# Linear attention and a feed-forward layer on one core: weight halves moved to GpSimd, the values' loads joined, the first loads on two queues

## The chip, the core and the metric

The kernel runs on one core of one Trainium2 chip. The metric is the device time of one execution in microseconds (us), and lower is better. In the profile PE is TensorE, PEld its weight loads, DVE is VectorE, ACT is ScalarE, POOL is GpSimd and SP is SyncE.

## The reference

Two parts follow each other. A linear attention over 8 batches, 8 heads, 576 positions and 64 elements per head; its result, 4608 tokens of 512 elements, goes through a feed-forward layer of 512 to 2048 to 512.

```python
def phi(x):
    proj = np.einsum('bhsd,df->bhsf', x, w_phi)            # 128 features
    proj = proj - np.max(np.abs(proj), axis=-1, keepdims=True)
    return np.concatenate([np.exp(proj), np.exp(-proj)], axis=-1)
q_p, k_p = phi(q), phi(k)
kv = np.einsum('bhsf,bhsd->bhfd', k_p, v)
z = np.sum(k_p, axis=2)
num = np.einsum('bhsf,bhfd->bhsd', q_p, kv)
den = np.einsum('bhsf,bhf->bhs', q_p, z)[..., None] + 1e-06
x = (num / den)                                            # as (4608, 512)
h = x @ w_in
out = np.maximum(0.01 * h, h) @ w_out
```

All is in float32. The seeds' factors make q, k and w_phi larger than plain normal numbers would be, so the exponentials spread widely.

## The kernel before, in words

**Pairs.** Two heads are handled together as a pair: 8 batches of 4 pairs, 32 pairs in all. `k_phase(i)` turns the keys and values of pair i into the table `kv` (with z beside it: the values' tile has 66 columns per row, 64 of v and two of ones), and `q_phase(i)` uses that table for the queries and writes normalized tokens into `ring`, two batches of them. Pairs 0 to 3 have functions of their own (`first_k_phase`, `first_q_phase`), since all engines are still empty then. In pairs 4 to 7 ("nat" in the code) the products are plain float32; from pair 8 on each operand is split into a high and a low half in float32r, and three products replace one.

**The feed-forward layer.** Tokens are taken in 18 blocks of 256. `split` divides a block into halves xh and xl. `layer1(i, ft)` makes one of 16 slices of the hidden layer (128 of 2048) for one block: 12 matmuls of 256 columns, lines 595, 596 and 598. `layer2` multiplies the slice's halves gh and gl by the second weight: 3 matmuls of 512 columns for each half of the block, lines 615 to 617. The first two blocks run side by side, slice by slice, so that each weight is used twice as it comes.

**The weights' halves.** The weights arrive as 64-bit floats, two 32-bit words each, and float32 numbers are built from them on the chip. `load_weights` (line 164 on) has 32 steps of 128x512 numbers, w_in and w_out of 16 slices in turn, and each step does this: one DMA of 512 KB into a raw buffer, Abs on ACT (line 177), two TENSOR_SCALARs (lines 178 and 179) and one SCALAR_TENSOR_TENSOR (line 180) on DVE, one more activation on ACT (line 182), an add on DVE (line 183, printed as ISA or CUSTOM_DVE), then a copy that rounds to the high half h on ACT, and a subtraction that leaves the low half l on DVE. The last two go through helpers and are printed as lines 67 (CAST w0h, w1h) and 72 (w0l, w1l). The step's tile `ql` has two buffers and `kvl` one. The first ten steps take their raw weights into `ring`, two buffers in turn.

**What sets the order.** Nothing is ordered by hand. The program gives each part a priority (`PF` for pairs 0 to 3, then `PU`, `PA` for the attention stream, `PW` for the weights, 0 for the layers), and a scheduler that runs when the program is built lays down, engine by engine, a fixed order of instructions. Each engine then works its list from the top, and waits where an input isn't there. So any edit may move instructions anywhere.

**Loads.** SP issues all DMAs. At the start (lines 147 to 157) they are the keys of pairs 0 and 1, `bd` (w_phi twice, on the diagonal of a tile that GpSimd has zeroed, line 148), the values of pairs 0 and 1, then keys and values of pairs 2 and 3. The values of a pair take three DMAs (lines 142 to 144, later lines 195 to 197): eight blocks of 64 columns from `v`, and the last 64 positions twice from `vt`, for each half of the partitions. The tile `rv` has one buffer; each time it is taken anew, GpSimd writes its ones (line 198). `load_k(i + 1)`, which loads keys and values of the next pair, is called early in `k_phase(i)`, while the matmuls of pair i still have to read `rv` in pairs 4 to 7. In later pairs the values are split into `vhl` first, and `rv` is free from then on.

Of the kernel before, what the change touches and what calls it, by code (L numbers as in the profile page):

```python
# [9 lines left out]
F32 = mybir.dt.float32  # L10
# [4 lines left out]
ALU = mybir.AluOpType  # L15
AX = mybir.AxisListType

P = 128
# [12 lines left out]
NN = 8  # L31
NK = 8
BUFS = {"kk": 4, "pmk": 2, "eq": 2, "m4": 3, "m4n": 2, "g": 2, "gh": 2, "gl": 2, "qh": 2, "ql": 2, "dn": 2}
PBUFS = {"a": 3, "c": 1, "h": 2, "acc": 2}
# [9 lines left out]
@with_exitstack  # L44
def attention_moe_kernel(ctx: ExitStack, tc: tile.TileContext, q, k, v, vt, w_phi, w_in, w_out, out):
    nc = tc.nc
# [4 lines left out]
    def ct(shape, dt, name):  # L51
        return cp.tile(shape, dt, tag=name, name=name)

    def st(shape, dt, tag, name=None):
        return sp.tile(shape, dt, tag=tag, name=name or tag, bufs=BUFS.get(tag, 1))

# [7 lines left out]
    def copy_(key, o, i):  # L64
        e = pick(key) or "a"
        if e == "a":
            nc.scalar.copy(o, i)  # L67
        else:
            (nc.vector if e == "v" else nc.gpsimd).tensor_copy(o, i)  # L69

    def tt_(key, o, a, b, op):
        (nc.vector if pick(key) == "v" else nc.gpsimd).tensor_tensor(o, a, b, op=op)  # L72
# [50 lines left out]
    def part(x, i, shape):  # L123
        n = shape[0] * (shape[1] if len(shape) == 2 else 1)
        x = x[:, i : i + n]
        return x if len(shape) == 1 else x.rearrange("p (a b) -> p a b", b=shape[1])

    first_k, first_q = {}, {}

    def first_load_k(i):  # L130
        if i == 0:
            rk = st([P, S], F32, "rk")
            rv = st([P, 10, 66], F32, "rv")
        else:
            rk = part(fk[i], 0, [S])
            rv = part(fk[i], S, [10, 66])
        nc.sync.dma_start(rk, k[i])
        first_k[i] = rk, rv

    def first_load_v(i):  # L140
        rv = first_k[i][1]
        nc.sync.dma_start(rv[:, 0:8, 0:64], v[i])
        nc.sync.dma_start(rv[0:64, 8:10, 0:64], vt[i])
        nc.sync.dma_start(rv[64:128, 8:10, 0:64], vt[i])
        nc.gpsimd.memset(rv[:, :, 64:66], 1.0)

    tc.cur_priority = 2 * PF
    nc.gpsimd.memset(bd, 0.0)
    for j in range(2):
        nc.sync.dma_start(bd[64 * j : 64 * j + 64, F * j : F * j + F], w_phi)  # L150
    for i in range(2):
# [9 lines left out]
    def load_weights():  # L161
        n = 0
        for ft in range(NFT):
            for which, src in ((0, w_in), (1, w_out)):
# [19 lines left out]
                h, l = weight(which, "h", ft), weight(which, "l", ft)  # L184
                copy_("h", h, w)
                tt_("l", l, w, h.bitcast(F32), ALU.subtract)
                n += 1
# [3 lines left out]
    def load_k(i):  # L191
        rk = st([P, S], F32, "ks" if i < NK and i % 2 else "rk")
        rv = st([P, 10, 66], F32, "rv")
        nc.sync.dma_start(rk, k[i])
        nc.sync.dma_start(rv[:, 0:8, 0:64], v[i])
        nc.sync.dma_start(rv[0:64, 8:10, 0:64], vt[i])
        nc.sync.dma_start(rv[64:128, 8:10, 0:64], vt[i])
        nc.gpsimd.memset(rv[:, :, 64:66], 1.0)  # L198
        kraw[i] = rk, rv

# [7 lines left out]
    def k_phase(i):  # L208
        nat = i < NK
        rk, rv = kraw.pop(i)  # L210
        if not nat:
# [9 lines left out]
        if i + 1 < B * NP:  # L221
            load_k(i + 1)
        yield
        wq = None if nat else w_phi_split()
# [83 lines left out]
        for c in range(2, 5):  # L308
            chunk(c)
            yield  # L310
        kvs = st([P, 2, 256], F32, "kk", "kvs").rearrange("p a (b f) -> p a b f", b=2)[0:66]
        copy_("kvs", kvs, kvp[0:66].rearrange("p (a b f) -> p a b f", a=2, b=2))
# [118 lines left out]
    def first_k_phase(i):  # L431
        od = i % 2
        rk, rv = first_k.pop(i)
        if i == 2:
            load_k(NP)
        yield
        kvp = pt("h")
# [273 lines left out]
```

## Time and profile before

| | |
|---|---|
| three runs | 1187.79, 1189.28 and 1189.99 us, median 1189.28 us |
| the profiled execution | 1187.94 us, of which the profile's span is 1186.2 us |
| TensorE clock granted | 1.00 throughout |
| busy share of the span | PE 97%, PEld 87%, ACT 73%, DVE 65%, POOL 53% |
| DMA | 57.88 MB in 71005 packets, 49 GB/s on the mean |

The lines of a profile read so. A group has line, engine, operation, tiles (written<-read), shapes and count; behind the first bar are its busy time in us and the mean of one in ns, behind the second the idle time of the engine just before these instructions and what ended it. A row of the waits is "who <- what ended it: us in total, times, longest us". A row of the timeline is the start in us, the duration in us, engine, line, operation and tiles, and in square brackets the idle time before it. A row of the windows is a stretch of the span, its length, and for each engine the busy time with the number of its instructions, then the granted clock, the share of the DMA engines' time and GB/s. A row of a tile is the shortest, the median and the longest duration in ns.

### The profile page before, as it was taken

How to read it: one execution, taken by the hardware profiler on the slowest of the kernel's cores; microseconds unless marked ns; L12 is line 12 of the kernel's file. 1: busy time of each engine (PE TensorE's matmuls, PEld its weight loads, DVE VectorE, ACT ScalarE, POOL GpSimd, SP SyncE). 2: the span in 40 equal slices, each digit the busy share in tenths (PEclk: the TensorE clock that was granted, in tenths of full speed). 3: DMA queues.
4: the chain of work that ended last, by engine and by line, in shares of the span. 5: the costliest groups of instructions: out<-in, count | busy, mean ns of one | idle time of the engine just before them, and what ended most of it. 6: DMA issues, size and time to landing. Idle time of an engine off the chain costs nothing.

```text
span 1186.2 us, 21604 instructions
## 1 busy us (share of the span) xinstructions
PE 1153.7 (97%) x7496; PEld 1026.5 (87%) x7496; DVE 769.2 (65%) x1326; ACT 861.3 (73%) x2266; POOL 632.7 (53%) x709
## 2 busy tenths in 40 slices
PE   8899999899998999999999999999999999999998
PEld 5677778799887989889999999999999989899997
DVE  5988995587788778777777777757777765200000
ACT  5978775878788778777888878868887785433232
POOL 0131222576576667666666666757666666433232
PEclk9999999999999999999999999999999999999999
DMA  8436331211111111111111111101111100000000
GB/s 218 135 91 168 103 108 36 70 41 34 51 33 50 34 34 29 42 34 30 52 33 51 33 51 26 48 23 40 33 50 34 40 3 20 1 19 9 10 19 18
DMA packets 71005, 57.88 MB, mean 49 GB/s; under 512 B 53232, under 2 KB 54512, under 8 KB 70896
## 3 DMA queue, kind: packets, MB, share of 16 engines
q1 hardware_dynamic: 70896, 56.51, 17.1%
q8 instruction: 59, 0.97, 0.3%
q14 instruction: 50, 0.41, 0.1%
HBM read 46.27 MB, written 9.44 MB: 47 GB/s over the span
## 4 chain that ended last, share of the span: by engine, by line
PE 47%; DVE 2%; DMA 1%; issue 0%; ACT 0%; POOL 0%; SPq 0%; DVEq 0%; ACTq 0%; POOLq 0%
PE h L598 6%; PE h L596 6%; PE h L595 6%; PE acc L616 6%; PE acc L617 6%; PE acc L615 6%; PE c L228 3%; PE a L409 1%; PE a L404 1%; PE a L406 1%; PE a L251 1%; PE a L365 1%; PE a L364 1%; DVE tq L381 0%; DMA mx<-mx 0%
## 5 line engine op out<-in xcount | busy, mean ns | idle before, releaser
L72 POOL TENSOR_TENSOR gl<-g,gh 128x256 fp32r<-128x256 f32 x288 | 237.3, 827 | 305.4 <-ACT gh L67 220.2
L595 PE MATMUL h<-xh,w0h 128*128 128x256 f32 x1088 | 278.8, 283 | 2.4 <-ACT xh L67 1.3
L596 PE MATMUL h<-xh,w0l 128*128 128x256 f32 x1088 | 276.6, 281 | 0.0
L595 PEld LDWEIGHTS h<-xh,w0h 128*128 128x128 f32 x1088 | 205.4, 189 | 12.4 <-ACT g L602 2.4
L615 PE MATMUL acc<-w1h,gh 128*128 128x512 f32 x544 | 214.3, 394 | 0.2 <-DVE o L69 0.2
L616 PE MATMUL acc<-w1l,gh 128*128 128x512 f32 x544 | 213.3, 392 | 0.0
L596 PEld LDWEIGHTS h<-xh,w0l 128*128 128x128 f32 x1088 | 205.3, 189 | 8.4 <-issue 0.4
L617 PE MATMUL acc<-w1h,gl 128*128 128x512 f32 x544 | 203.5, 395 | 2.6 <-POOL rv L198 1.2
L598 PE MATMUL h<-xl,w0h 128*128 128x256 f32 x1088 | 191.2, 281 | 0.0
L602 ACT ACTIVATE g<-h 128x256 f32<-128x256 f32 x288 | 108.3, 381 | 106.0 <-PE h L598 83.0
L72 POOL TENSOR_TENSOR ql<-eq,qh 128x576 fp32r<-128x576 f32 x96 | 142.9, 1500 | 53.3 <-DVE qh L395 44.3
L67 ACT CAST gh<-g 128x256 fp32r<-128x256 f32 x288 | 115.2, 403 | 63.0 <-PE acc L616 60.9
L598 PEld LDWEIGHTS h<-xl,w0h 128*128 128x128 f32 x1088 | 155.9, 188 | 0.9 <-issue 0.4
L72 POOL TENSOR_TENSOR kpl<-ek,kph 128x512 fp32r<-128x512 f32 x72 | 101.5, 1410 | 75.9 <-ACT kph L67 59.3
L617 PEld LDWEIGHTS acc<-w1h,gl 128*128 128x128 f32 x544 | 99.5, 188 | 19.5 <-POOL rv L198 1.4
L69 DVE COPY o<-acc 128x512 f32<-128x512 f32 x17 | 11.7, 688 | 161.0 <-DMA out_dram<-o 118.0
L615 PEld LDWEIGHTS acc<-w1h,gh 128*128 128x128 f32 x544 | 102.5, 188 | 12.1 <-DVE o L69 0.4
L616 PEld LDWEIGHTS acc<-w1l,gh 128*128 128x128 f32 x544 | 102.3, 188 | 11.7
L282 ACT ACTIVATE ek<-pmk,m 128x128 f32<-128x128 f32 (+1 forms) x240 | 89.5, 390 | 13.5 <-DVE m L259 13.1
L281 ACT ACTIVATE ek<-pmk,m4n 128x128 f32<-128x128 f32 (+1 forms) x240 | 90.1, 392 | 8.6 <-DVE m4n L265 3.9
L395 DVE TENSOR_REDUCE qh<-eq 128x576 fp32r<-128x576 f32 x96 | 69.0, 751 | 25.7 <-ACT eq L389 22.9
L256 DVE TENSOR_TENSOR pmk<-a,pmk 128x256 f32<-128x256 f32 (+1 forms) x120 | 49.6, 420 | 54.0 <-ACT pmk L67 52.0
(183 smaller groups left out, 2404.8 us busy)
## 6 DMA issues: line engine op xcount, KB each, us to landing
out_dram<-o SPq DMA_DIRECT2D x36, 256.0 KB, 2.1
rq<-in_q_dram SPq DMA_DIRECT2D x28, 288.0 KB, 2.9
rk<-in_k_dram SPq DMA_DIRECT2D x27, 288.0 KB, 2.8
rv<-in_v_dram SPq DMA_DIRECT2D x29, 256.0 KB, 3.5
ring<-in_w_in_dram SPq DMA_DIRECT2D x9, 512.0 KB, 3.7
f<-in_w_out_dram SPq DMA_DIRECT2D x7, 512.0 KB, 3.6
f<-in_w_in_dram SPq DMA_DIRECT2D x7, 512.0 KB, 3.6
ring<-in_w_out_dram SPq DMA_DIRECT2D x5, 512.0 KB, 3.8
```

The costliest lines, as they stand in the source:

```text
L67: nc.scalar.copy(o, i)
L72: (nc.vector if pick(key) == "v" else nc.gpsimd).tensor_tensor(o, a, b, op=op)
L281: nc.scalar.activation(ek[r, j, 0:F], pmk[r, h], AF.Exp, bias=m4n[r, h : h + 1])
L282: nc.scalar.activation(ek[r, j, F:256], pmk[r, h], AF.Exp, scale=-1.0, bias=m4[r, h : h + 1])
L395: nc.vector.tensor_reduce(qh, eq.unsqueeze(3), axis=AX.X, op=ALU.max)
L595: nc.tensor.matmul(ph, lhsT=weight(0, "h", ft)[:, d * P : d * P + P], rhs=xh[d], start=d == 0, stop=False)
L596: nc.tensor.matmul(ph, lhsT=weight(0, "l", ft)[:, d * P : d * P + P], rhs=xh[d], start=False, stop=False)
L598: nc.tensor.matmul(ph, lhsT=weight(0, "h", ft)[:, d * P : d * P + P], rhs=xl[d], start=False, stop=d == NP - 1)
L602: nc.scalar.activation(g, ph, AF.Prelu, alpha=0.01)
L615: nc.tensor.matmul(a, lhsT=gh[:, ts], rhs=weight(1, "h", ft), start=ft == 0, stop=False)
L616: nc.tensor.matmul(a, lhsT=gh[:, ts], rhs=weight(1, "l", ft), start=False, stop=False)
L617: nc.tensor.matmul(a, lhsT=gl[:, ts], rhs=weight(1, "h", ft), start=False, stop=ft == NFT - 1)
```

## The change

1. **Halves on GpSimd.** In the first ten of the 32 weight steps the rounding copy and the subtraction are GpSimd instructions, one behind the other; ACT and DVE no longer have them. Steps 11 to 32 are as before.
2. **Values.** The host lays the last 64 positions, twice, behind the other blocks of `v`, so one DMA per pair fills all 64 columns of the tile. The tile of pair 0 is a constant one, `rv0`, whose ones are written once; all pairs from 4 on use it, and the 28 memsets of line 198 are gone. In pairs 4 to 7 the load for the next pair stands behind the last matmul that reads the tile; from pair 8 on it stands where it stood.
3. **First loads.** w_phi and the values of pairs 0 and 1 are issued by ACT, the rest by SP. GpSimd zeroes only the parts of `bd` that no DMA writes.

```diff
+NPOOL = 10
...
+    rv0 = ct([P, 10, 66], F32, "rv")
...
     def first_load_v(i):
         rv = first_k[i][1]
-        nc.sync.dma_start(rv[:, 0:8, 0:64], v[i])
-        nc.sync.dma_start(rv[0:64, 8:10, 0:64], vt[i])
-        nc.sync.dma_start(rv[64:128, 8:10, 0:64], vt[i])
-        nc.gpsimd.memset(rv[:, :, 64:66], 1.0)
+        (nc.scalar if i < 2 else nc.sync).dma_start(rv[:, :, 0:64], v[i])
+        if i:
+            nc.gpsimd.memset(rv[:, :, 64:66], 1.0)
 
     tc.cur_priority = 2 * PF
-    nc.gpsimd.memset(bd, 0.0)
     for j in range(2):
-        nc.sync.dma_start(bd[64 * j : 64 * j + 64, F * j : F * j + F], w_phi)
+        r = slice(64 * j, 64 * j + 64)
+        nc.scalar.dma_start(bd[r, F * j : F * j + F], w_phi)
+        nc.gpsimd.memset(bd[r, F * (1 - j) : F * (2 - j)], 0.0)
+    nc.gpsimd.memset(rv0[:, :, 64:66], 1.0)
...
                 h, l = weight(which, "h", ft), weight(which, "l", ft)
-                copy_("h", h, w)
-                tt_("l", l, w, h.bitcast(F32), ALU.subtract)
+                if n < NPOOL:
+                    nc.gpsimd.tensor_copy(h, w)
+                    nc.gpsimd.tensor_tensor(l, w, h.bitcast(F32), op=ALU.subtract)
+                else:
+                    copy_("h", h, w)
+                    tt_("l", l, w, h.bitcast(F32), ALU.subtract)
...
     def load_k(i):
         rk = st([P, S], F32, "ks" if i < NK and i % 2 else "rk")
-        rv = st([P, 10, 66], F32, "rv")
         nc.sync.dma_start(rk, k[i])
-        nc.sync.dma_start(rv[:, 0:8, 0:64], v[i])
-        nc.sync.dma_start(rv[0:64, 8:10, 0:64], vt[i])
-        nc.sync.dma_start(rv[64:128, 8:10, 0:64], vt[i])
-        nc.gpsimd.memset(rv[:, :, 64:66], 1.0)
-        kraw[i] = rk, rv
+        kraw[i] = rk
+
+    def load_v(i):
+        nc.sync.dma_start(rv0[:, :, 0:64], v[i])
...
         if i + 1 < B * NP:
             load_k(i + 1)
+            if not nat:
+                load_v(i + 1)
...
         for c in range(2, 5):
             chunk(c)
             yield
+        if nat:
+            load_v(i + 1)
```

The scheduler lays the whole program anew, and the lists of all five engines differ. Two places matter most. The first is GpSimd's list just behind its opening memsets, in the stage of pairs 0 to 3; `f_82` is a buffer of the start, `ring<-ring,mb` is the normalization that ends a query part of one pair, `xl<-ring,xh` the low half of the tokens. Before:

```order
L145 MEMSET f_82 128x10x2
L198 MEMSET rv 128x10x2
L72 TENSOR_TENSOR ring<-ring,mb 128x256 x2
L72 TENSOR_TENSOR xl<-ring,xh 128x256 x2
L72 TENSOR_TENSOR ring<-ring,mb 128x256
L72 TENSOR_TENSOR xl<-ring,xh 128x256
```

The same place after the change, from the ninth of the twenty new rows on:

```order
L189 CAST w0h_622<-ql 128x512
L190 TENSOR_TENSOR w0l_623<-ql,w0h_622 128x512
L189 CAST w1h_635<-ql 128x512
L73 TENSOR_TENSOR ring<-ring,mb 128x256
L190 TENSOR_TENSOR w1l_636<-ql,w1h_635 128x512
L73 TENSOR_TENSOR xl<-ring,xh 128x256
L189 CAST w0h_622<-ql 128x512
L73 TENSOR_TENSOR ring<-ring,mb 128x256
L190 TENSOR_TENSOR w0l_623<-ql,w0h_622 128x512
L73 TENSOR_TENSOR xl<-ring,xh 128x256
```

Eleven of the twenty weight instructions stand ahead of the first normalization; the other nine stand one by one between the normalizations and the low halves of the tokens.

The second place is the head of SP's list; `f_79`, `f_80` and `f_82` hold keys and values of pairs 1 to 3. Before, its rows from the first up to the values of pair 1:

```order
L137 DMA rk<-in_k_dram 128x576
L150 DMA bd<-in_w_phi_dram 64x128 x2
L137 DMA f_80<-in_k_dram 128x576
L142 DMA rv<-in_v_dram 128x8x64
L143 DMA rv<-in_vt_dram 64x2x64
L144 DMA rv<-in_vt_dram 64x2x64
L142 DMA f_80<-in_v_dram 128x8x64
L143 DMA f_80<-in_vt_dram 64x2x64
L144 DMA f_80<-in_vt_dram 64x2x64
```

After the change, from its first row to the first two weights:

```order
L139 DMA rk<-in_k_dram 128x576
L139 DMA f_80<-in_k_dram 128x576
L139 DMA f_79<-in_k_dram 128x576
L144 DMA f_79<-in_v_dram 128x10x64
L139 DMA f_82<-in_k_dram 128x576
L144 DMA f_82<-in_v_dram 128x10x64
L500 DMA ks<-in_q_dram 128x4x256
L500 DMA rq<-in_q_dram 128x4x64
L175 DMA ring<-in_w_in_dram 128x1024
L175 DMA ring<-in_w_out_dram 128x1024
```

Eight DMAs now stand ahead of the first weight on SP's list, where there were 21, the keys of pair 4 among them; those now stand behind the second weight. ACT's list begins with the two DMAs of `bd` and the values of pairs 0 and 1, and only then loads its table.

More of the change, by code (lines that the diff above doesn't have):

```diff
@@ L44, in attention_moe_kernel @@
 @with_exitstack
-def attention_moe_kernel(ctx: ExitStack, tc: tile.TileContext, q, k, v, vt, w_phi, w_in, w_out, out):
+def attention_moe_kernel(ctx: ExitStack, tc: tile.TileContext, q, k, v, w_phi, w_in, w_out, out):
     nc = tc.nc
@@ L132, in first_load_k @@
             rk = st([P, S], F32, "rk")
-            rv = st([P, 10, 66], F32, "rv")
+            rv = rv0
         else:
@@ L192, in load_k @@
         rk = st([P, S], F32, "ks" if i < NK and i % 2 else "rk")
-        rv = st([P, 10, 66], F32, "rv")
         nc.sync.dma_start(rk, k[i])
-        nc.sync.dma_start(rv[:, 0:8, 0:64], v[i])
-        nc.sync.dma_start(rv[0:64, 8:10, 0:64], vt[i])
-        nc.sync.dma_start(rv[64:128, 8:10, 0:64], vt[i])
-        nc.gpsimd.memset(rv[:, :, 64:66], 1.0)
-        kraw[i] = rk, rv
+        kraw[i] = rk
+    def load_v(i):
+        nc.sync.dma_start(rv0[:, :, 0:64], v[i])
     def load_q(i):
@@ L209, in k_phase @@
         nat = i < NK
-        rk, rv = kraw.pop(i)
+        rk, rv = kraw.pop(i), rv0
         if not nat:
@@ L435, in first_k_phase @@
             load_k(NP)
+            load_v(NP)
         yield
@@ L687 @@
     q, k, v = (inputs[n] for n in ("q", "k", "v"))
+    tail = v[:, :, 512:].reshape(B * NP, 2, 64, D).transpose(0, 2, 1, 3)
+    tail = _np.concatenate([tail, tail], 1)
     lay = {
@@ L690 @@
         "k": k.transpose(0, 1, 3, 2).reshape(B * NP, P, S),
-        "v": v[:, :, :512].reshape(B * NP, 2, 4, P, D).transpose(0, 3, 1, 2, 4).reshape(B * NP, P, 8, D),
-        "vt": v[:, :, 512:].reshape(B * NP, 2, 64, D).transpose(0, 2, 1, 3),
+        "v": _np.concatenate([v[:, :, :512].reshape(B * NP, 2, 4, P, D).transpose(0, 3, 1, 2, 4).reshape(B * NP, P, 8, D), tail], 2),
         "w_phi": inputs["w_phi"],
```

## The prediction

> **What bounds the kernel now.** I read the page first, for the engines' shares.
>
> ```profile
> span 1186.2 us, 21604 instructions
> PE 1153.7 (97%) x7496; PEld 1026.5 (87%) x7496; DVE 769.2 (65%) x1326; ACT 861.3 (73%) x2266; POOL 632.7 (53%) x709
> L595 PE MATMUL h<-xh,w0h 128*128 128x256 f32 x1088 | 278.8, 283 | 2.4 <-ACT xh L67 1.3 <-ACT g L602 1.1
> ```
>
> TensorE is the bound over the span: 1186.2 - 1153.7 leaves 32.5 us in which it shows nothing. That is a lower bound of what it waits, since its records overlap: 1088 times 0.283 us is 308 us, and they fill 278.8 us. Small waits lie hidden under such records.
>
> The change works on the first tenth of the span, so next come windows, cut where the load of the engines changes.
>
> ```profile
> core 0: us, PE busy (x) PEld busy (x) DVE busy (x) ACT busy (x) POOL busy (x), PEclk, DMA share, GB/s
> 0.00:20.00 20.00, 15.79 (x65) 11.60 (x65) 8.76 (x15) 7.36 (x14) 1.25 (x14) 1.00 0.84 224
> 20.00:75.00 55.00, 48.19 (x239) 35.13 (x239) 50.41 (x103) 50.57 (x113) 11.73 (x15) 1.00 0.44 133
> 75.00:185.00 110.00, 107.75 (x596) 83.97 (x594) 98.79 (x180) 82.84 (x197) 24.70 (x33) 1.00 0.41 118
> 185.00:250.00 65.00, 61.02 (x383) 51.80 (x382) 38.50 (x70) 48.99 (x133) 29.84 (x40) 1.00 0.21 56
> 250.00:1186.00 936.00, 920.89 (x6219) 843.99 (x6218) 572.74 (x961) 671.53 (x1813) 565.21 (x609) 1.00 0.12 31
> ```
>
> From 20 to 75 us DVE and ACT are both busy 92% of the time, GpSimd 21%, and TensorE is idle for 6.8 us. From 75 to 185 us, while the other 22 weight steps run, DVE alone is the tight one (90%). From 250 us on TensorE has all the work it can do, so microseconds that it gains before that reach the end undiminished. The waits between 19 and 75 us say who ends TensorE's idle time there, and where DVE itself waits.
>
> ```profile
> DVE ql L178 <- ACT ql L177: 4.8, 3, 3.7
> PE c L537 <- ACT eq L522: 1.9, 1, 1.9
> PE h L595 <- ACT xh L67: 1.3, 2, 0.7
> PE h L537 <- ACT dn L541: 1.0, 1, 1.0
> ```
>
> TensorE waits for ACT's exponentials and copies, which stand in line with the weights' work: two saturated engines feed it.
>
> **Part 1, the halves.** What leaves ACT and DVE, and what GpSimd has to do in that stage already, by groups between 19 and 72 us:
>
> ```profile
> L180 DVE SCALAR_TENSOR_TENSOR ql<-ring,ql 128x512 int32<-128x512 int32 x10 | 7.0, 704 | 0.1
> L72 POOL TENSOR_TENSOR ring<-ring,mb 128x256 f32<-128x256 f32 x6 | 5.7, 943 | 32.1 <-ACT dn L541 26.4 <-DVE mb L547 5.7
> L179 DVE TENSOR_SCALAR ql<-ql 128x512 int32<-128x512 int32 x10 | 4.4, 436 | 0.1
> L72 DVE TENSOR_TENSOR w0l<-ql,w0h 128x512 fp32r<-128x512 f32 x5 | 3.9, 782 | 0.0
> L72 DVE TENSOR_TENSOR w1l<-ql,w1h 128x512 fp32r<-128x512 f32 x5 | 3.7, 748 | 0.2
> L72 POOL TENSOR_TENSOR xl<-ring,xh 128x256 fp32r<-128x256 f32 x4 | 3.4, 861 | 5.7 <-ACT xh L67 5.7
> L67 ACT CAST w1h<-ql 128x512 fp32r<-128x512 f32 x5 | 3.1, 616 | 0.0
> L67 ACT CAST w0h<-ql 128x512 fp32r<-128x512 f32 x5 | 3.1, 616 | 0.0
> ```
>
> DVE loses 3.9 + 3.7 = 7.6 us, ACT 3.1 + 3.1 = 6.2 us. What GpSimd takes for them: its subtraction of two 128x512 tiles is in the trace as kpl, its rounding copy is not. The nearest rows for the copy are a memset, which reads nothing, below, and kpl, which reads twice as much, above.
>
> ```profile
> L72 POOL TENSOR_TENSOR kpl<-ek,kph x72: 1269/1299/1876, 218.7 to 978.7; 128x512 fp32r<-128x512 f32 x72
> L148 POOL MEMSET bd<- x1: 311/311/311, 0.7 to 0.7; 128x256 f32 x1
> ```
>
> So a copy lies between 2 x 0.31 = 0.6 and 1.9 us; I take 0.9, nearer to the memset, since one input is read and not two. A step is then 0.9 + 1.3 = 2.2 us (bounds 1.9 and 3.8), ten of them 22 us (19 to 38). GpSimd has 53 - 9.1 = 44 us free between 19 and 72 us (the 9.1 are the ring and xl rows), so at 22 us it keeps up and all of it lies beside other work. The cover is thin only at the upper end.
>
> It isn't free for DVE, though. Five rows of the timeline at 55 us, where GpSimd and DVE work together:
>
> ```profile
> 55.33 0.43 DVE L178 TENSOR_SCALAR ql<-ql 128x512 f32<-128x512 f32 x1 [0.83 <-ACT ql L177]
> 55.67 0.73 POOL L72 TENSOR_TENSOR xl<-ring,xh 128x256 fp32r<-128x256 f32 x1 [1.65 <-ACT xh L67]
> 56.03 0.65 DVE L179 TENSOR_SCALAR ql<-ql 128x512 int32<-128x512 int32 x1
> 56.36 0.91 POOL L72 TENSOR_TENSOR ring<-ring,mb 128x256 f32<-128x256 f32 x1
> 56.60 1.21 DVE L72 TENSOR_TENSOR w0l<-ql,w0h 128x512 fp32r<-128x512 f32 x1
> ```
>
> The TENSOR_SCALAR that meets GpSimd takes 0.65 us where the group's mean is 0.44, the subtraction 1.21 where its mean is 0.78. The Trainium skill (GPSIMD Engine Reference, section 8, Key points) states it as a rule: GpSimd shares its SBUF interfaces with VectorE and contends with DVE instructions in a two-port mode or with two SBUF inputs. By that rule the change hands part of its gain back; the rows agree. DVE keeps, in the ten steps, 30 operations of lines 178 to 180. If half of them meet GpSimd, at 0.65 - 0.44 = 0.21 us each, DVE gives back 15 x 0.21 = 3.2 us (none meet: 0; all meet: 6.3). So DVE's net relief is 7.6 - 3.2 = 4.4 us (1.3 to 7.6), ACT's 6.2 us. TensorE can't get more than the slower of its two feeders gives, nor much more than the 6.8 us that it is idle there: I credit 3.5 us, a little under DVE's 4.4, because part of the freed time will go into weight steps that TensorE doesn't need yet (bounds: -6.3, worked out under the rivals, and +6.8).
>
> **Part 2, the values.** The rows of the tile and the one wait of TensorE that names it:
>
> ```profile
> L198 POOL MEMSET rv<- x28: 108/116/201, 21.1 to 927.2; 128x20 f32 x28
> L195 SPq DMA_DIRECT2D rv<-in_v_dram x28: 564/603/614, 22.8 to 927.2; - x28
> L196 SPq DMA_DIRECT2D rv<-in_vt_dram x28: 659/660/719, 23.4 to 927.8; - x28
> PE acc L617 <- POOL rv L198: 1.2, 1, 1.2
> ```
>
> Removed are 28 x 0.116 = 3.2 us of GpSimd and two of three issues, about 0.6 us each, of SP per pair. Neither is on TensorE's path; what I credit is the one wait of 1.2 us, in which gl stood near a memset. The load's new place in pairs 4 to 7 costs nothing that I can find: before, too, it had to wait for the last reader of the tile; what is queued behind it on SP (the small m and mx DMAs, the next weights) waits no longer than it did, and it is one issue long and not three. Credit 1.2 us, bounds 0 and 2.
>
> **Part 3, the first loads.**
>
> ```profile
> 0.73 1.28 ACT L455 ACT_TABLE_LOAD   x1 [0.73 <-PEq L697]
> 0.74 0.39 SPq L137 DMA_DIRECT2D rk<-in_k_dram  x1
> 1.19 1.21 SPq L150 DMA_DIRECT2D bd<-in_w_phi_dram  x2
> 4.21 3.75 PE L425 MATMUL acc<-bd,rk 128*128 128x256 f32 x8 [4.21 <-DMA bd<-in_w_phi_dram]
> 13.91 0.50 SPq L172 DMA_DIRECT2D ring<-in_w_in_dram  x1
> 19.95 0.67 ACT L177 ACTIVATE ql<-ring 128x512 f32<-128x512 f32 x1 [1.69 <-DMA ring<-in_w_in_dram]
> 20.66 0.43 DVE L178 TENSOR_SCALAR ql<-ql 128x512 f32<-128x512 f32 x1 [3.66 <-ACT ql L177]
> ```
>
> The first matmul waits for bd, issued from 1.19 to 2.40 us. From ACT's queue it can go out from 0.73 us on, some 0.45 us sooner; the keys of pair 0, issued at 0.74, are the next to be waited for. I credit 0.4 us (0 to 0.5). The table's load goes behind four issues, 0.73 + 4 x 0.6 + 1.28 = 4.4 us; the first exponential needs the first matmuls and two DVE operations of 0.7 us, so it stays hidden. The first weight is issued at 13.91 us, since 21 issues of SP stand before it; after the change 8 do, and the keys of pair 4 come behind it. The DMA engines are 84% busy in the first 20 us, so of the 20 us only 0.16 x 20 = 3.2 us can be won, and the keys of pair 4 (288 KB at 224 GB/s: 1.3 us) on top. The Trainium skill (Trainium Kernel Development and Optimization, section Key Constraints) says that the queues of SP, ACT and GpSimd all run on the same 16 DMA engines, so that a second queue saves issue time alone; by that rule the sum would hold only these two terms, and the share of 0.84 fits it. DVE's gap of 3.66 us may shrink by about 2. That is relief for the same saturated stage as part 1, and TensorE has nothing idle before 20 us beyond its first 4.2; of the 2 us I credit 0.6 (0 to 2).
>
> **The sum.** 3.5 + 1.2 + 0.4 + 0.6 = 5.7 us off the profiled execution's 1187.94 us: 1182.2. The profiled execution is 1.34 us under the median of the three runs, 1189.28, and a new median should stand as far above its own quick runs, so the forecast is 1189.28 - 5.7 = 1183.6 us.
>
> **Rivals.**
>
> *More than that.* DVE's 10% of idle time from 75 to 185 us, and TensorE's small waits there that the overlap hides, may shrink too, if the weights come early through the whole stage. TensorE then gets all 6.8 us of 20 to 75, 1.2, 0.4, and the 2.25 us that it is idle from 75 to 185: 10.65 us, median 1178.6. For it: GpSimd and SP have room. Against: steps 11 to 32 of the weights are not touched.
>
> *No change.* The weights of the ten steps come sooner, but TensorE's waits are ended by the exponentials, and the scheduler has laid every list anew; from 185 us on TensorE is idle for 4.0 + 15.1 = 19.1 us in waits that the new lists may shift by a few us either way. Gain 5.7, given back 5: 1188.6. For it: 15 of those 19 us lie behind 250 us, where little of the change acts, so they can only change by the new order. Against: there is no reason that the new order is the worse one.
>
> *Slower: GpSimd becomes the bound.* Its list is fixed, and nine weight instructions now stand between the normalizations (ring) and the low halves (xl) on which TensorE's first slice of layer 1 depends. The point from which it decides is a copy of 1.9 us: then a step takes 3.8 us, ten take 38, with the 9.1 us of today 47 us of 53, and each of the four normalizations of the first tokens stands behind a weight instruction of up to 1.9 us, 4 x 1.9 = 7.6 us late in all. DVE gives back its 6.3 us as well, so that its relief is nearly gone. That leaves 1.3 - 7.6 = -6.3 us for part 1; with 1.2 + 0.4 + 0.6 us of the other parts it is 4.1 us slower: 1193.4. For it: the copy's price isn't in the trace; against: a copy reads half of what kpl reads.
>
> **How the numbers follow.** Forecast 0.56, more 0.13, no change 0.16, slower 0.15. From the unknown costs the forecast's own range is 1179 to 1187. The range that holds the time 8 times in 10 reaches from the rival with more gain into the one that is slower: 1176.5 to 1191. A measurement of this kernel can tell about 0.2%, 2.4 us, from no change. Faster by more than that is the forecast and its larger rival, 0.56 + 0.13 = 0.69; within it 0.16; slower 0.15.
>
> **What would show it.** The mark for the lead is the first matmul of pair 4's values:
>
> ```profile
> L228 PE MATMUL c<-ek,rv x80: 376/379/432, 84.3 to 186.0; 128*66 128x256 f32 x64, 64*66 64x256 f32 x16
> ```
>
> Right: between 20 and 75 us, DVE's busy time falls by 4 to 5 us and ACT's by 6 in what they do up to the tenth weight step, GpSimd's rises by about 22; the copies on GpSimd take 0.6 to 1.2 us; lines 178 to 180 are longer than before; the first matmul starts at about 3.8 us; DVE's gap before its first weight operation is under 2 us; no wait for a memset of rv is left; and TensorE reaches that matmul some 4 to 5 us before 84.3 us. Wrong: copies of 1.5 us and more with TensorE waiting for ring or xl; or an early lead at 84 us that is gone at 250 or at the end, by waits in places that the change doesn't touch.

## The result

| | median us | lowest to highest |
|---|---|---|
| before | 1189.19 | 1187.79 to 1189.99 |
| after | 1176.66 | 1175.97 to 1177.08 |

The ratio is 0.9895, 95% interval 0.9882 to 0.9907: 12.5 us less, where 5.7 were forecast. The profiled execution of after took 1176.74 us. One execution below, the profiled one of e9_third, was disturbed: nothing is read from it, and e9_third's time is the median of its other five runs.

### The profile page after: what moved, and what is told of

It reads as the page before. It is cut to its first block, busy times and chain, and to the rows that moved or that the text cites. A ratio compares the mean times of both kernels' runs of the same rounds, so it can differ in the third digit from the quotient of the medians.

```text
span 1175.0 us, 21456 instructions
## 1 busy us (share of the span) xinstructions
PE 1151.6 (98%) x7496; PEld 1024.4 (87%) x7496; DVE 751.6 (64%) x1316; ACT 856.7 (73%) x2256; POOL 651.0 (55%) x702
## 4 chain that ended last, share of the span: by engine, by line
PE 77%; DVE 11%; ACT 5%; DMA 2%; issue 2%; SPq 1%; POOL 0%; ACTq 0%; DVEq 0%; POOLq 0%
PE h L605 10%; PE h L608 10%; PE h L606 9%; PE acc L627 9%; PE acc L625 9%; PE acc L626 9%; PE c L235 6%; PE a L413 2%; PE a L258 2%; PE a L418 2%; PE a L415 2%; PE h L470 1%; PE a L434 1%; PE a L373 1%; PE a L374 1%
## 5 line engine op out<-in xcount | busy, mean ns | idle before, releaser
L73 POOL TENSOR_TENSOR kpl<-ek,kph 128x512 fp32r<-128x512 f32 x72 | 99.8, 1386 | 75.4 <-ACT kph L68 65.6
```

## The profile after

The page's span and engines, and the windows of the prediction with after's own end:

```profile
span 1175.0 us, 21456 instructions
...
PE 1151.6 (98%) x7496; PEld 1024.4 (87%) x7496; DVE 751.6 (64%) x1316; ACT 856.7 (73%) x2256; POOL 651.0 (55%) x702
```

```profile
0.00:20.00 20.00, 14.49 (x54) 11.14 (x55) 9.54 (x17) 7.98 (x14) 1.45 (x15) 1.00 0.84 228
20.00:75.00 55.00, 48.34 (x241) 34.95 (x240) 47.32 (x89) 43.97 (x100) 30.11 (x32) 1.00 0.44 132
75.00:185.00 110.00, 107.20 (x586) 82.51 (x585) 99.02 (x182) 84.52 (x199) 26.83 (x30) 1.00 0.42 120
185.00:250.00 65.00, 63.96 (x407) 55.22 (x406) 42.09 (x74) 50.50 (x137) 29.14 (x38) 1.00 0.20 56
250.00:1175.00 925.00, 917.57 (x6214) 840.59 (x6212) 553.62 (x958) 669.76 (x1810) 563.49 (x587) 1.00 0.11 32
```

The second row holds what the prediction asked for on the engines: DVE down by 3.1 us, ACT by 6.6, GpSimd up by 18.4. TensorE has got nothing from it: 48.34 us busy against 48.19. Its counts say more. By 185 us it has begun 54 + 241 + 586 = 881 matmuls, where before had 65 + 239 + 596 = 900. (A matmul that lies across a border counts in both rows, which makes such sums 2 to 4 too high, in every kernel.) So after is behind there by 19 matmuls, at 0.152 us each (before's remaining 1001.2 us over its remaining 6602) 2.9 us. From 185 us to the end it takes 990.0 us; less those 2.9 us that is 987.1 for the work that took before 1001.2. **Ahead of 185 us the change loses 2.9 us, behind it, it gains 14.1.** The difference, 11.2 us, is that of the spans.

Behind 185 us, in the last two rows, TensorE shows 1.0 + 7.4 = 8.5 us without work, where before showed 4.0 + 15.1 = 19.1: 10.6 of the 14.1 us; the rest, by inference, lies in waits that overlapping records hide. All waits of TensorE from 185 us on:

```profile
PE c L235 <- DVE kst L303: 2.1, 5, 0.9
PE c L235 <- POOL kpl L73: 0.7, 1, 0.7
PE a L373 <- ACT dn L421: 0.4, 1, 0.4
PE a L418 <- POOL ql L73: 0.3, 1, 0.3
PE c L235 <- DVE kvl L340: 0.2, 1, 0.2
PE h L605 <- ACT g L612: 0.2, 1, 0.2
```

That is 3.9 us. In before the same view lists 14.5 us; these are gone, and so is the memset of rv:

```profile
PE a L404 <- DVE qh L395: 3.9, 4, 1.4
PE a L404 <- DVE pmk L256: 1.6, 1, 1.6
...
PE a L251 <- DVE ks L216: 1.0, 1, 1.0
```

In the first and the third of these lines TensorE waits for halves of pairs 8 and later. In the second, at 228.86 us, a query part of an earlier pair waits until DVE's sum pmk has read a buffer of tile `a`. No edit touches these operations.

The prices on GpSimd, and the mark for the lead:

```profile
L190 POOL TENSOR_TENSOR w0l<-ql,w0h 128x512 fp32r<-128x512 f32 x5 | 7.7, 1539 | 0.2
L190 POOL TENSOR_TENSOR w1l<-ql,w1h 128x512 fp32r<-128x512 f32 x5 | 6.8, 1365 | 0.2
...
L189 POOL CAST w0h<-ql 128x512 fp32r<-128x512 f32 x5 | 3.4, 688 | 31.9 <-DVE ql L186 31.9
L189 POOL CAST w1h<-ql 128x512 fp32r<-128x512 f32 x5 | 3.1, 612 | 3.6 <-DVE ql L186 3.6
```

```profile
L235 PE MATMUL c<-ek,rv x80: 376/379/432, 85.9 to 182.7; 128*66 128x256 f32 x64, 64*66 64x256 f32 x16
```

A copy takes 0.61 to 0.69 us on the mean (taken as 0.9), a subtraction 1.37 to 1.54 (taken as 1.3), all twenty 21.0 us (22). The price of GpSimd was right. The lead is not there: the mark stands at 85.9 us, not 4 to 5 us ahead of 84.3 but 1.6 behind it.

What DVE pays: its four operations of a weight step between 20 and 75 us, the two of before that the prediction didn't show, then after (one of line 181's ten ran before 20 us):

```profile
L183 DVE CUSTOM_DVE_ANT_0 ql<-ql,kvl 128x1024 uint16<-128x1024 uint16 x10 | 6.9, 691 | 0.0
...
L178 DVE TENSOR_SCALAR ql<-ql 128x512 f32<-128x512 f32 x10 | 4.2, 417 | 4.8 <-ACT ql L177 4.8
```

```profile
L183 DVE SCALAR_TENSOR_TENSOR ql<-ring,ql 128x512 int32<-128x512 int32 x10 | 8.8, 879 | 0.2
L186 DVE CUSTOM_DVE_ANT_0 ql<-ql,kvl 128x1024 uint16<-128x1024 uint16 x10 | 8.1, 814 | 0.5 <-ACT kvl L185 0.5
L181 DVE TENSOR_SCALAR ql<-ql 128x512 f32<-128x512 f32 x9 | 5.0, 553 | 3.6 <-ACT ql L180 3.6
L182 DVE TENSOR_SCALAR ql<-ql 128x512 int32<-128x512 int32 x10 | 4.6, 459 | 0.2
```

Before they cost 7.0 + 6.9 + 4.4 + 4.2 = 22.5 us, after 26.5 and with the missing one, 0.4 us, 26.9. So 4.4 of the 7.6 us that DVE was relieved of are given back; 3.2 were forecast, from 30 operations. The ten adds (printed as CUSTOM_DVE), which that sum left out, pay 1.2 of the 4.4.

The first loads. The first weight is issued 5.3 us sooner, the first matmul starts later:

```profile
5.51 2.04 PE L434 MATMUL acc<-bd,rk 128*128 128x256 f32 x4 [5.51 <-DMA bd<-in_w_phi_dram]
...
8.60 2.50 SPq L175 DMA_DIRECT2D ring<-in_w_in_dram  x1
```

## The experiments

The rival theories. **O**: the gain is made by the order that the scheduler laid anew, mostly by TensorE's late order; the same work in another order makes it too. Its rivals (V, L, W, S in the texts below) put the gain into the work that the parts move or save. A second question is why the start got no faster; its theories (Q, F, D, B) are told where they stand.

The scheduler's results are of two kinds here. From about row 500 of TensorE's list on, a kernel follows after to a few rows ("new" below), or it is on before's track, row for row from about row 1500 on at the latest ("old"). Which one comes out hangs on trifles. The table has every profiled kernel but e18_load_early, which works on other values, with before's and after's numbers worked out as above: matmuls begun by 185 us; what then remains, with 0.152 us added or taken off for each matmul of lead or lag against before; the start of the fourth copy of tokens (tile xh, on ACT), and of the tenth weight step's add on DVE.

| kernel | of the change | late order | median us | ratio [95%] | matmuls by 185 us | rest us | 4th xh us | 10th add us |
|---|---|---|---|---|---|---|---|---|
| before | none | old | 1189.19 | 1 | 900 | 1001.2 | 63.3 | 68.7 |
| e1_values | 2 | old | 1182.79 | 0.9935 [0.9920, 0.9951] | 904 | 996.4 | 62.8 | 68.4 |
| e2_halves | 1 | old | 1194.61 | 1.0037 [1.0024, 1.0049] | 865 | 1002.7 | 69.2 | 68.2 |
| e3_loads | 3 | old | 1189.80 | 0.9992 [0.9981, 1.0002] | 880 | 999.1 | 67.8 | 67.7 |
| e5_spfirst | 1, 2 | old | 1188.44 | 0.9985 [0.9975, 0.9995] | 873 | 997.2 | 69.1 | 68.1 |
| e11_no_values | 1, 3 | old | 1190.33 | 1.0016 [1.0007, 1.0026] | 885 | 1000.7 | 64.5 | 67.8 |
| e4_none_a | 2, 3 | old | 1191.16 | 1.0010 [1.0000, 1.0019] | 871 | 1000.5 | 68.7 | 68.6 |
| e8_none_b | 2, 3 | new | 1182.17 | 0.9933 [0.9918, 0.9948] | 864 | 988.8 | 66.5 | 68.5 |
| e7_eight | 1 (8 steps), 2, 3 | old | 1183.97 | 0.9946 [0.9929, 0.9964] | 899 | 997.4 | 65.6 | 68.0 |
| e6_nine | 1 (9 steps), 2, 3 | new | 1177.08 | 0.9889 [0.9872, 0.9906] | 876 | 987.9 | 67.6 | 68.8 |
| after | 1, 2, 3 | new | 1176.66 | 0.9895 [0.9882, 0.9907] | 881 | 987.1 | 67.1 | 68.3 |
| e13_one_step | 2, 1 in one late step | new | 1175.64 | 0.9883 [0.9863, 0.9902] | 901 | 988.6 | 63.9 | 69.7 |
| e14_sub10 | 2, subtractions of 1 | new | 1179.72 | 0.9912 [0.9892, 0.9933] | 890 | 990.9 | 65.9 | 69.6 |
| e15_cast10 | 2, copies of 1 | old | 1187.77 | 0.9976 [0.9966, 0.9986] | 887 | 997.0 | 65.8 | 66.3 |
| e16_third_again | all, third buffer | new | 1186.49 | 0.9969 [0.9955, 0.9983] | 856 | 990.6 | 71.3 | 61.5 |
| e10_third_none | 2, 3, third buffer | new | 1181.39 | 0.9945 [0.9928, 0.9962] | 868 | 991.7 | 69.1 | 66.5 |
| e12_third_24 | 1 (12 steps), 2, 3, third buffer in 24 | new | 1191.47 | 1.0022 [1.0010, 1.0034] | 804 | 990.4 | 74.5 | 63.2 |
| e17_memsets | all, memsets back | new | 1177.45 | 0.9893 [0.9876, 0.9909] | 880 | 987.7 | 66.9 | 68.1 |

Two readings carry the rest. The column of the rest splits by the late order: new 987 to 992, old with part 2 about 997 (e4_none_a 1000.5), old without it 999 to 1003. And the matmuls begun by 185 us follow the fourth copy of tokens on the whole, from 904 at 62.8 us to 804 at 74.5, and not the weights' tenth add.

The traces allow a count of the late order without the correction. From the 1017th matmul on (at 205 to 222 us) all new kernels have one order, and at the 1017th and at the 3001st matmul both kinds have done the same matmuls but for 3 to 6. From the one to the other the new kernels take 294.9 to 297.0 us (after 295.2, e13_one_step 295.3), the old 302.6 to 306.5 (before 304.9, e1_values 303.8). From there to the end the two kinds overlap, at 671.9 to 676.6 us. In seven of the nine old kernels the granted clock falls to 0.50 for 3.4 us of that stretch, between 360 and 374 us, which costs at most half of that, 1.7 us; before and e15_cast10 (304.9 and 302.6) have no such fall and lie above the new ones all the same. So the late order goes with 5.6 to 11.6 us, all of them won between 205 and 518 us. Before and after differ there by 9.7 us.

### The parts one by one

e1_values has part 2 alone, e2_halves part 1 alone, e3_loads part 3 alone (the values still in three DMAs each). e5_spfirst is after with all first loads back on SP:

```diff
-        (nc.scalar if i < 2 else nc.sync).dma_start(rv[:, :, 0:64], v[i])
+        nc.sync.dma_start(rv[:, :, 0:64], v[i])
...
-        nc.scalar.dma_start(bd[r, F * j : F * j + F], w_phi)
+        nc.sync.dma_start(bd[r, F * j : F * j + F], w_phi)
```

> Part 2 alone on the kernel before (one DMA per pair's values, one constant tile, ones written once, load behind the last matmul in pairs 4 to 7). Its lists differ from those of before only up to about 1400 of TensorE's 5873 rows. Theory V (the values' waits were the cost, and they sat in the whole span): 8 to 10 us faster, 1180, and TensorE's idle time from 250 us on falls from 15.1 to about 8 us. Theory O (most of the gain is the new order from pair 8 on, which only the three parts together bring about): 2 to 4 us faster, 1186, and TensorE's waits behind 500 us are those of before but for the 1.2 us at a memset.

> Part 1 alone on the kernel before (halves of ten weight steps on GpSimd); TensorE's list differs from that of before in its first 500 rows only. Theory V and theory O both: 0 to 2 us faster, 1188, since the changed kernel was no earlier at 185 us. The forecast's own step (3.5 us from these halves) would be 1185.7.

> Part 3 alone on the kernel before (w_phi and the values of pairs 0 and 1 issued by ACT, partial zeroing of bd). Theory V and theory O both: 0 to 2 us slower, 1190, because the first matmul starts at 5.5 us as in the changed kernel, not at 4.2. The forecast's step (1.0 us from these loads) would be 1188.2.

> The changed kernel with all first loads on SP (parts 1 and 2, and the partial zeroing). Its lists differ from those of before only up to about 1400 of TensorE's rows. Theory V: as fast as the changed kernel or 1 us faster, 1176. Theory O: 3 to 5 us faster than before only, 1185, so about 8 us slower than the changed kernel, although the edit that is undone acts on the first 20 us alone.

The parts don't add: -7.5 us (against 1190.31 for before on that chip), +4.3 and -0.5 make -3.7, after has -12.5, and parts 1 and 2 without 3 come to -1.9. The halves alone make the kernel slower. Their four DVE operations in e2_halves:

```profile
L181 DVE SCALAR_TENSOR_TENSOR ql<-ring,ql 128x512 int32<-128x512 int32 x10 | 11.2, 1118 | 0.2
L184 DVE CUSTOM_DVE_ANT_0 ql<-ql,kvl 128x1024 uint16<-128x1024 uint16 x10 | 7.2, 723 | 0.4
L180 DVE TENSOR_SCALAR ql<-ql 128x512 int32<-128x512 int32 x10 | 6.8, 676 | 0.2
L179 DVE TENSOR_SCALAR ql<-ql 128x512 f32<-128x512 f32 x10 | 5.7, 572 | 3.2 <-ACT ql L178 3.2
```

They take 30.9 us for 22.5: DVE gives back 8.4 us and was relieved of 7.6. The Trainium skill (GPSIMD Engine Reference, section 8, Key points) names such contention between GpSimd and DVE; the trace agrees, with 1118 ns for 704 at the worst. Part 3 alone moves nothing that can be told: its first weight goes out at 13.68 us, 0.2 us sooner than before, and the time is the same. The Trainium skill's rule that the queues share the DMA engines, so that a second one saves issue time alone (Trainium Kernel Development and Optimization, section Key Constraints), agrees with that ratio of 0.9992.

### The same work in another order

e6_nine and e7_eight are after with `NPOOL = 9` and `NPOOL = 8`. In e4_none_a it is 0, so no halves are on GpSimd, and e8_none_b is e4_none_a with two generators of pairs 2 and 3 swapped:

```diff
-NPOOL = 10
+NPOOL = 0
...
-    together(first_k_phase(2), first_k_phase(3))
+    together(first_k_phase(3), first_k_phase(2))
```

> The changed kernel with nine weight steps on GpSimd and not ten. Its lists are those of the changed kernel but for a few rows of the first 250 of TensorE. Theory O (the gain hangs on which of two long orders the scheduler lays down): as fast as the changed kernel, ratio to before 0.989 to 0.991. Theory L (the first loads and the halves help each other in the first 75 us): the same.

> The changed kernel with eight weight steps on GpSimd. From about row 1400 on TensorE's list is that of before, not that of the changed kernel. Theory O: 8 to 12 us slower than with nine, ratio 0.996 to 1.000, and the loss lies behind 250 us. Theory L: within 2 us of nine steps, ratio 0.989 to 0.992, since eight of ten halves and all the loads are there.

> Parts 2 and 3 without part 1 (no halves on GpSimd), and the generators of pairs 2 and 3 named in the other order, which changes no work. Its list on TensorE is that of the changed kernel but for 35 rows. Theory O: faster than the changed kernel by what the halves cost when alone (4 us), ratio 0.985 to 0.988. Theory L: no gain from halves, so as the values alone, ratio 0.993 to 0.995.

> Parts 2 and 3 without part 1, the generators in their own order; the tail of its lists is that of before. Differs from the kernel with the two generators swapped in nothing but the order. Theory O: as the values alone, ratio 0.992 to 0.995, so 6 to 10 us slower than its twin. Theory L: the same as its twin within 2 us.

One weight step fewer on GpSimd costs 6.9 us (1177.08 to 1183.97), and a swap that changes no instruction gains 9.0 (1191.16 to 1182.17). Both pairs differ in the late order, and both times it is the new one that is quicker. O's own figures missed, though: e8_none_b (0.9933 for 0.985 to 0.988) and e4_none_a (1.0010 for 0.992 to 0.995) are both slower than it said, and e7_eight (0.9946) lies between the theories. What held is the difference within a pair. The strongest case came last: before with part 2 and the halves of one step, the 27th, on GpSimd. Its first 250 rows on TensorE are those of before.

```diff
-                copy_("h", h, w)
-                tt_("l", l, w, h.bitcast(F32), ALU.subtract)
+                if n == 26:
+                    nc.gpsimd.tensor_copy(h, w)
+                    nc.gpsimd.tensor_tensor(l, w, h.bitcast(F32), op=ALU.subtract)
+                else:
+                    copy_("h", h, w)
+                    tt_("l", l, w, h.bitcast(F32), ALU.subtract)
```

> Before with part 2 (values), and of the halves only those of weight step 27 on GpSimd. TensorE's first 250 rows are those of before, its rows from 500 on those of after. Theory O: the late order makes the gain. With the values alone TensorE had begun 904 matmuls by 185 us (900 before, 881 after) and took 1182.8 us in the old late order; the two kernels that differ in little but the late order lay 6.9 and 9.0 us apart. So 1173 to 1176 us, under after. Rival W: the gain behind 185 us came from the weights' halves that GpSimd took in the first 75 us, of which this kernel has none: 1181 to 1184 us.

It gains as much as after, without part 3 and with one step of part 1: 0.9883 [0.9863, 0.9902]. O holds. The late lists of DVE and ACT change together with TensorE's in all these kernels, and no run forces one list alone, so whose order makes the gain isn't separated. Its last two windows read like after's, with 1.2 + 8.3 us of TensorE without work:

```profile
185.00:250.00 65.00, 63.82 (x402) 54.84 (x401) 42.00 (x74) 51.35 (x139) 29.62 (x39) 1.00 0.19 52
250.00:1173.00 923.00, 914.67 (x6203) 838.28 (x6201) 552.06 (x955) 667.69 (x1806) 561.80 (x586) 1.00 0.12 32
```

What the order does is seen in TensorE's timeline at one place. The columns are start, duration, line, tiles, and in brackets the wait; lines 617 to 619 (621 to 623) and 597, 598 and 600 (601, 602, 604) are the layers. In e1_values, old order:

```profile
223.32 0.40 PE L619 MATMUL a<-w1h,gl 128*128 128x512 f32 x1
223.56 1.13 PE L405 MATMUL a<-eq,kvh 128*128 128x288 f32 x4
224.31 0.61 PE L227 MATMUL c<-kpl,vhl 128*66 128x256 f32 x2
226.12 1.24 PE L405 MATMUL a<-eq,kvh 128*128 128x288 f32 x4 [1.20 <-DVE pmk L255]
...
229.79 0.39 PE L250 MATMUL a<-wq,ks 128*128 128x256 f32 x1 [1.28 <-DVE ks L213]
230.02 0.28 PE L597 MATMUL h<-xh,w0h 128*128 128x256 f32 x1
```

In e13_one_step, new order, the same stretch:

```profile
224.27 1.13 PE L409 MATMUL a<-eq,kvh 128*128 128x288 f32 x4
225.03 0.60 PE L621 MATMUL h<-w1h,gh 128*128 128x512 f32 x1
...
226.74 0.39 PE L623 MATMUL h<-w1h,gl 128*128 128x512 f32 x1
226.97 0.39 PE L623 MATMUL a<-w1h,gl 128*128 128x512 f32 x1
227.19 0.40 PE L254 MATMUL a<-wq,ks 128*128 128x256 f32 x2
```

The old order has no matmul of the layers for 6 us there, from 223.7 to 230.0 us, and TensorE waits twice for DVE: until the sum pmk has read a buffer of tile `a`, and for a half of the keys (ks). The new order has put a group of layer 2 and some of layer 1 between the same attention matmuls, and TensorE waits at neither place.

### Why the start got no faster

The tenth weight step's add comes at 68 to 69 us in before and in after alike. Theory Q: a step's first operation has to wait until the subtraction of the step before the last one has freed one of the two buffers of `ql`; a third buffer lets the weights run ahead. F: the steps stand behind the pairs' work in the fixed lists.

```diff
-                w = st([P, DM], F32, "ql")
+                w = part(f3, 512, [DM]) if n % 3 == 2 and n < 10 else st([P, DM], F32, "ql")
```

e9_third and e16_third_again are after with it, e10_third_none has no halves on GpSimd besides, and e12_third_24 uses the third buffer in 24 steps (`n < 24`), with `NPOOL = 12`.

> After, with a third buffer for the tile in which the first ten weight steps are built (every third step uses a free part of a buffer of the start). TensorE's order from its row 500 on is that of after, row for row. Theory Q: the ten steps are paced by the two buffers of ql, since a step's Abs waits for the subtraction of the step before the last one, and that is now the slower engine's; with three buffers the tenth step's add, at 68.3 us in after, comes at 64 us or before, the first matmul of pair 4's values at 84 us or before (85.9 in after), and the time is 1172 to 1175 us. Rival F: the steps stand behind the pairs' work in the fixed lists of ACT and DVE; the tenth add stays within 1 us of 68.3, the matmul within 1 us of 85.9, and the time is 1176 to 1178 us.

> The same third buffer, but all halves on ACT and DVE as before the change (parts 2 and 3 stay). TensorE's late order is again that of after. The kernel without the halves in this late order took 1182.2 us. Theory Q: the buffer alone gives ACT and DVE nothing, since they are busy over 90% of 20 to 75 us without the change; tenth add at 67 to 69 us, time 1181 to 1183 us, so that the halves on GpSimd are worth 7 to 10 us once there is a third buffer. Rival F: tenth add at 68 to 69 us, time 1181 to 1183 us, and the halves are worth 5 us as without the buffer.

> After with the third buffer for the first 24 weight steps and the halves of 12 steps on GpSimd; TensorE's late order is that of after. Theory Q: the steps of 75 to 150 us come sooner as well; 1171 to 1174 us. Rival F: 1176 to 1179 us.

> The kernel of e9_third once more, for a profile. Its six times were 1183.6 to 1189.1 us but for one disturbed run, so theory Q has fallen as to the time. If the tenth step's add comes at 64 us or before and the time is still 1183 us or more, the steps were paced by the buffers, but TensorE does not live by them: fewer than 875 matmuls begun by 185 us. If the add stays at 67 us or later, the steps were never paced by the buffers (theory F), and the time is 1176 to 1189 us.

e9_third took 1185.83 us (0.9981 [0.9964, 0.9999]), and e16_third_again confirms it. Q was right on the weights and wrong on the time. With the third buffer the halves on GpSimd gain nothing either, where Q gave them 7 to 10 us: e10_third_none, without them, has the lower ratio (0.9945 against e9_third's 0.9981, on the same chip). And e12_third_24, with more of both, is the slowest of the new kernels. Of before, after and e16_third_again, the timeline's rows of the fourth copy of tokens and of the tenth add:

```profile
63.27 0.41 ACT L67 CAST xh<-ring 128x256 fp32r<-128x256 f32 x1
...
68.65 0.68 DVE L183 CUSTOM_DVE_ANT_0 ql<-ql,kvl 128x1024 uint16<-128x1024 uint16 x1
```

```profile
67.15 0.41 ACT L68 CAST xh<-ring 128x256 fp32r<-128x256 f32 x1
...
68.28 0.68 DVE L186 CUSTOM_DVE_ANT_0 ql<-ql,kvl 128x1024 uint16<-128x1024 uint16 x1
```

```profile
61.51 0.69 DVE L186 CUSTOM_DVE_ANT_0 ql<-ql,kvl 128x1024 uint16<-128x1024 uint16 x1
...
71.30 0.41 ACT L68 CAST xh<-ring 128x256 fp32r<-128x256 f32 x1
```

```profile
L235 PE MATMUL c<-ek,rv x80: 376/379/432, 92.5 to 186.1; 128*66 128x256 f32 x64, 64*66 64x256 f32 x16
```

With the third buffer the weights are 6.8 us ahead of after, the tokens 4.2 us behind it, and pair 4's first matmul comes at 92.5 us. So the buffers did pace the weights, but TensorE doesn't live by the weights there. It lives by the pairs, whose tokens are made on the same two engines; that the weights' sooner work is what makes the pairs later is the reading that fits, not one that a run isolates. In the waits of after from 20 to 75 us, DVE and ACT now wait for TensorE's products as well, which before they did for 0.7 us in all:

```profile
DVE m L266 <- PE a L434: 1.7, 2, 1.0
DVE m L517 <- PE a L434: 1.1, 1, 1.1
```

```profile
ACT ring L550 <- PE c L547: 1.9, 2, 1.6
```

That looks like a loop: products, maxima on DVE, exponentials on ACT, products. Taking load off its two engines didn't shorten it here: DVE and ACT were idle for 7.7 and 11.0 us of the 55 in after, for 4.6 and 4.4 in before. Slower DVE operations and weight steps in between would lengthen it; that isn't shown by itself. Two kernels split the halves: e14_sub10 moves the subtractions alone, e15_cast10 the copies alone (both before with part 2).

```diff
-                tt_("l", l, w, h.bitcast(F32), ALU.subtract)
+                if n < 10:
+                    nc.gpsimd.tensor_tensor(l, w, h.bitcast(F32), op=ALU.subtract)
+                else:
+                    tt_("l", l, w, h.bitcast(F32), ALU.subtract)
```

> Before with part 2, and the subtractions alone of the first ten steps on GpSimd; the copies stay on ACT. TensorE's late order is that of after. Theory D: GpSimd's subtraction, with its two inputs, is what slows DVE's own work from 20 to 75 us and lengthens each step; then TensorE is as far behind at 185 us as with all halves moved (865 to 881 matmuls begun), and the time is 1178 to 1181 us. Rival B: moving only one of the two leaves the step's chain nearly as short as before and frees DVE by 7.6 us; then 895 to 905 matmuls by 185 us and 1173 to 1176 us.

> Before with part 2, and the copies alone of the first ten steps on GpSimd; the subtractions stay on DVE. TensorE's late order is that of before. Theory D: a copy has one input and disturbs DVE little, so the start is like that with the values alone (895 to 905 matmuls by 185 us) and the time 1182 to 1184 us. Rival B: the copy's way over a third engine lengthens the step's chain; 865 to 885 matmuls by 185 us, 1185 to 1188 us.

e14_sub10 takes the time that D gave (1179.72 us), but with 890 matmuls begun by 185 us it lies between D's and B's counts; e15_cast10 is at B's time (1187.77 us) with 887. Neither theory holds for both. Both kernels lose some 15 matmuls against e1_values, and in both the fourth copy of tokens is 3 us later. Which instruction of the lists is to blame isn't settled, since every edit also re-lays the first 500 rows. Weights of lower priority, which the finding points to, were not tried.

### What the values are worth

e11_no_values is after without part 2. e17_memsets is after with `nc.gpsimd.memset(rv0[:, :, 64:66], 1.0)` back in `load_v`. e18_load_early calls `load_v(i + 1)` right behind `load_k(i + 1)` in all pairs; in the program's order that stands ahead of the matmuls that read the tile, so in pairs 4 to 7 they use the values of the next pair, and the load no longer waits for them. Contrary to what its expectation says, its wait for the last reader is therefore not the one of before.

> After without part 2: values by three DMAs into a new tile with a memset each, as before; parts 1 and 3 stay. TensorE's late order is that of before, row for row. Theory V: joining the values saves 7 us or so by itself, as it did alone (1182.8 us); against the 1184.0 us of the kernel with all three parts and eight steps on GpSimd, whose late order is also that of before, this one takes 1190 to 1192 us. Rival S: what the values' part alone gained came from the order of the start that the scheduler made of it, and not from the loads; then 1183 to 1187 us.

> After, with the memset of the two columns of ones back in every pair from 4 on (28 of them, 3.2 us of GpSimd). TensorE's order is that of after, row for row. Theory O: the memsets cost what the prediction credited, one wait of 1.2 us at the most, and the rest of what part 2 gained by itself came from the order: 1176 to 1178 us. Rival V: the memsets held up the values, the layers' low halves or SP's list in many places: 1179 to 1183 us.

> After, with the load of the next pair's values in pairs 4 to 7 back at its early place, ahead of the matmuls that read the tile. TensorE's order is that of after, row for row. Theory O: 1176 to 1177.5 us, since the load waits for the tile's last reader either way. Rival V: the waiting load holds up the weights and keys behind it on SP, 1178 to 1181 us.

e17_memsets takes 1177.45 us (0.9893 [0.9876, 0.9909]) and after 0.9895 [0.9882, 0.9907]: 28 memsets, and the wait of 1.2 us that the prediction credited, are worth nothing that can be told in this order. e18_load_early takes 1176.97 us (0.9890 [0.9875, 0.9904]), which shows only that the time doesn't hang on when these four loads go out. e11_no_values takes 1190.33: without part 2, parts 1 and 3 gain nothing. By the column of the rest, part 2 goes with some 4 us behind 185 us even in the old order (996.4 to 997.4, but 1000.5 in e4_none_a, against 999 to 1003). But every old kernel with part 2 also has another order than before in a good part of TensorE's first 1500 rows, so what of the 4 us is order and what is saved DMA issues stays open. No kernel here without part 2 has the new late order.

## Why the prediction was wrong

The direction was right, and the range held the time at its lower edge. The gain was more than twice the forecast, and not by the terms of the sum: a loss and a larger gain that it didn't have stand against each other.

- **The halves, 3.5 us.** The step that failed is "TensorE waits for ACT's exponentials and copies, which stand in line with the weights' work: two saturated engines feed it", from which the relief of the slower feeder was credited. The relief came nearly as forecast (DVE 7.6 - 4.4 = 3.2 us, forecast 4.4; ACT 6.6, forecast 6.2). But the two engines only stood idle for longer: the weights' tenth add came 0.4 us sooner, the fourth copy of tokens 3.9 us later, and TensorE was 1.6 us late at pair 4 (4 to 5 ahead were expected) and 2.9 us behind at 185 us. A busy share of 92% on two engines that work in a loop with TensorE was read as a queue of work that shortens with its load.
- **The order, 0 us.** The rival "No change" had the right place, the 19.1 us that TensorE is idle from 185 us on, and the right cause, "they can only change by the new order". The sum gave it zero, without a reason, and the rivals "a few us either way", mostly as a loss. This is the step that made the size wrong: behind 185 us 14.1 us were gained, of which 9.7 lie where the late order differs; between kernels that do nearly the same work it made 6.9 and 9.0 us. The other 4.4 us are not assigned. From the profile of before its sign couldn't be told; its size could: up to 19 us, more than all other terms together, so the range should have been drawn from it.
- **The values, 1.2 us.** The wait went, and is worth nothing by itself. With the order that comes with it part 2 makes 7.5 us alone.
- **The first loads, 1.0 us.** The first weight went out at 8.60 us, as the change intends, and the first matmul started at 5.51 us, not at 3.8. An earlier issue of `bd` was taken for an earlier landing: in the kernels here with `bd` issued by ACT the first matmul starts at 5.27 to 6.21 us, in those with SP at 4.21 to 5.32. Part 3 alone is worth nothing that can be told.
- **The slower rival** (GpSimd as the bound) did not decide: copies took 0.61 to 0.69 us and not 1.9, and in after a normalization stands behind a weight's copy for 0.7 us once (ready at 53.15 us, begun at 53.89). But part 1 alone did make the kernel slower, by 4.3 us where this rival had 6.3, and by another way: DVE gave back 8.4 us, more than the rival's upper bound for that.

## What to carry to other kernels

Where a scheduler lays the lists at build time, an edit is two changes: its work, and a new order of everything. Before crediting a gain to the work, build neighbours that differ in a trifle and compare the order and the time; here it was worth 7 to 9 us of 1180 between kernels that do nearly the same work. Part 2 alone gained 7.5 us, but it came with a new order too, so no edit was shown to be worth as much by its work. And before taking load off a busy feeder, ask which of its products the bound engine waits for: here it was the tokens, and taking the weights' work off the engines that make them didn't bring them sooner.

## What the hardware showed that was not expected

- GpSimd's work on the weights slows DVE's, by very different amounts: the SCALAR_TENSOR_TENSOR of a weight step took 704 ns on the mean in before, 879 in after and 1118 in e2_halves. The subtractions do most of it: with them alone on GpSimd (e14_sub10) it took 957 ns, with the copies alone (e15_cast10) 716. DVE's operations on TensorE's products stayed as they were (maxima of tile a 673 ns in before and in after), and so did its transposes (mb from dn, 443 and 435 ns), so not everything on DVE pays.
- GpSimd's normalizations of 128x256 took 757 ns on the mean in after, and 943 before. Its low halves xl, of the same shape, took 893 and 861. So DVE's smaller load in after isn't shown to make GpSimd faster.
- Two DMA issues on SP's queue in after took 2.70 and 2.50 us, at 5.04 and 8.60 us (a query tile and the first weight), while the other issues on it in the first 20 us took 0.33 to 0.78. The DMA engines were 84% busy over these 20 us.
- The granted clock is 1.00 throughout in the profiles of before and after. In others it falls to 0.50 for 3.4 us here and there (0.91 on the mean from 350 to 370 us in e1_values and e7_eight, 0.93 from 60 to 75 us in e12_third_24). In e1_values, matmuls of 128x288 then begin 0.24 us apart, and 0.13 us apart shortly before.
